# The portions in which feed-forward steps are given out, from unit 8 on, computed from a group's columns

## The chip, the core and the metric

The kernel runs on one core of a Trainium2 chip. It has five engines with a queue each: TensorE (PE in the profile; its weight loads are PEld), VectorE (DVE), ScalarE (ACT), GpSimd (POOL), and SyncE (SP), which here only issues DMAs. The metric is the device time of one execution in microseconds, as the median of several runs.

## What is computed

Attention first: 4 batches, 8 heads, 768 tokens, 48 features. Each head keeps a 48 x 48 state that is decayed by a gate for every feature and gains an outer product for every token:

```python
f = 1.0 / (1.0 + np.exp(-f_logit))
for t in range(S):
    state = f[:, :, t, :, None] * state + np.einsum('bhd,bhe->bhde', k[:, :, t], v[:, :, t])
    y[:, :, t] = np.einsum('bhd,bhde->bhe', q[:, :, t], state)
```

The result is read as x with 3072 tokens of 384 features and goes through a feed-forward network (FFN) with three first matrices of 384 x 768 and one output matrix of 768 x 384:

```python
h = np.maximum(np.maximum(x @ w1, x @ w2), x @ w3)
return h @ w_out
```

All of it is in float32.

## The kernel before

**Units and groups.** The attention works on units of 64 tokens of two batches, 24 in all (NU). Four units (GRP) make a group of 512 tokens (TOK), and the FFN works on one group at a time; its six groups are numbered 0 to 5. The FFN of a group can begin when the attention of its four units is done, so the FFN of group g runs beside the attention of group g + 1, and that of the last group runs alone at the end.

**A unit of attention.** `sigmoids(u)` (L308, ACT) gives the gates, `scan(u)` (L326, VectorE) their running products, `after(u)` and `before(u)` scale k and q by them to kh and qh (L337 and L348; from unit 8 on, POOL). `keys(u)` does nothing from unit 8 on; `keys_by_blocks(u, n)` (L379, VectorE) transposes kh in four parts, n = 0 to 3. `pairs(u)` multiplies kh and qh (L389, PE), and VectorE masks the product to `at` (L392). `values(u)` multiplies `at` with v (L408, PE) and calls `sums(u)` (L433, PE), which forms the new part of the state from the transposed keys and v; VectorE adds it (L441). `carry(n)` decays the state for the next unit (L354, POOL). `finish(u)` adds what the state gives (L503, PE) and copies the sum into the group's xT (L509, ACT). `pack` moves a part of xT to the place where the FFN reads it, with two DMAs (L522). The last two units (22 and 23) need no transposed keys and no L433.

**The FFN of a group.** `ffn(g)` is a generator. Its first part has twelve products of 512 columns, three matmuls each (L551); for each j there are two products, the first followed by a Relu on ACT (L749), the second by a maximum on VectorE into hm (L751). For the last three j, POOL forms sums of hm (L608, four operations for each j). The second part, `outputs_by_pairs`, has eleven steps, in each of which `into` runs twice with three matmuls of 192 columns (L623, 66 matmuls in all). Behind some of the steps ACT or VectorE copies or adds the result out of its bank (L634, L637, L639, L643, L646, L651, L659); the bank is used again by a later step. The stores of a group's outputs are issued by `store_late`, in the next group.

**What sets the order.** The program is written under a manual schedule: each engine runs its instructions in the order in which the Python code emits them. The loop over the units calls the parts of the attention and, between them, `fill(PART)` five times for each unit. `fill(ns)` adds ns to a budget and takes steps of the pending generators as long as the budget is over zero; each step yields its cost, which is columns times COLUMN = 4/2.4 ns. A step that overshoots leaves a negative budget for the next call, and what is left over when nothing is pending stays in the budget. At the start of a group, behind the first `fill` of unit 8, 12, 16 or 20, `finish` of the last unit of the group before is called, then `pack`, and then `ffn` of that group is appended to the pending generators; at the end the same is done for unit 23, and `fill(20000)`, `fill(9000)` and `fill(10 ** 6)` give out the rest. What is still pending from the group before comes first. The FFN of group 0 (`ffn_first`) is given out beside units 3 to 8.

From unit 11 on there are also checks of the weights' range on ACT (L276, L277, L279), two for each unit.

Of the kernel before, what the change touches and what calls it, by code (L numbers as in the profile page):

```python
# [55 lines left out]
def kernel(  # L56
# [18 lines left out]
    NK = DM // 128  # L75
    DFF = moe_w1.shape[1]
    NJ = DFF // 128
    GRP = 4
    TOK = GRP * UT
# [10 lines left out]
    def fast():  # L90
        ctx = ExitStack()
        with ctx:
# [95 lines left out]
            def load_v(u, queues=one):  # L188
                load_tokens(v_tiles[u % NLD], v, u, queues)
# [19 lines left out]
            def load_weights(count, done=0, queue=nc.sync):  # L209

                for n in range(len(raw_next), min(len(raw_next) + count, done + RAW, len(pieces))):
                    raw_next.append(n)
                    dst, src = pieces[n]
                    a = dst.shape[1]
                    if src.dtype != FP32:
                        raw[n] = new_raw(n)
                        dst, src = raw[n].rearrange("p (a c) -> p a c", a=a), src.bitcast(U32)
                    queue.dma_start(out=dst, in_=src.rearrange("(a p) c -> p a c", a=a))
# [308 lines left out]
            COLUMN = 4 / 2.4  # L527
# [59 lines left out]
            HJ, HD = NJ // 2, DM // 2  # L587
# [177 lines left out]
            def fill(ns):  # L765
                budget[0] += ns
                while budget[0] > 0 and pending:
                    try:
                        budget[0] -= next(pending[0])
                    except StopIteration:  # L770
                        pending.pop(0)
# [8 lines left out]
            def new_xT():  # L780
                return work.tile([128, HP, TOK], FP32, name="xT")

            CHECKS = 2 * GRP + 3
            STEP = NK * HALF * COLUMN
            PART = 2740

# [1 line left out]
            with tc.manual_schedule():  # L790
                load(0, both)
                load(1, (nc.scalar, nc.sync))
                load_v(0)
                load(2, one, "f")
                load_v(1)
                load(2, one, "kq")
                load(3)
                load_weights(3)
                load_v(2)
                load_v(3)  # L800
                load_weights(6)
                xT = new_xT()
                sigmoids(0)
                scan(0)
                after(0)
                before(0)
                sigmoids(1)
                keys(0)
                scan(1)
                after(1)  # L810
                pairs(0)
                before(1)
                sigmoids(2)
                busy(1)
                values(0)
                y_by_tokens(0)
                keys(1)
                sums(0)
                load(GRP)
                load_v(GRP)  # L820
                scan(2)
                after(2)
                pairs(1)
                x_of_tokens(0, xT)
                carry(2)
                before(2)
                sigmoids(3)
                busy(1)
                values(1)
                y_by_tokens(1)  # L830
                keys(2)
                sums(1)
                round_begin(0)
                round_end(0)
                x_of_tokens(1, xT)
                scan(3)
                pairs(2)
                round_begin(1)
                round_end(1)
                after(3)  # L840
                carry(3)
                round_begin(2)
                pending.append(ffn_first(xT))
                fill(STEP)
                before(3)
                values(2)
                fill(STEP)
                keys(3)
                sums(2)
                y_by_tokens(2)  # L850
                pairs(3)
                fill(STEP)
                x_of_tokens(2, xT)
                fill(STEP)
                values(3)
                fill(STEP)
                sums(3)
                fill(STEP)
                y_by_tokens(3)
                load(GRP + 1)  # L860
                load_v(GRP + 1)
                x_of_tokens(3, xT)
                sigmoids(GRP)
                scan(GRP)
                after(GRP)
                fill(2 * STEP)
                before(GRP)
                carry(GRP)
                fill(2 * STEP)
                for u in range(GRP, NU):  # L870
                    n = u + 1
                    fill(PART)
                    keys(u)
                    keys_by_blocks(u, 2)
                    if u > GRP:
                        finish(u - 1, xT)
                        if u % GRP == 3:
                            pack(0, 2, xT)
                        elif u % GRP == 0:
                            pack(3, 3, xT)  # L880
                    if u % GRP == 0:
                        if u > GRP:
                            pending.append(ffn(u // GRP - 1, xT))
                        xT = new_xT()
                    pairs(u)

                    if u + 2 < BY_ROWS:
                        load(u + 2)
                    if BY_ROWS <= u + 3 < NU and u % 2:
                        load(u + 3, one, "fkq" if u % GRP == 1 else "f")  # L890
                    if u + 2 < NU:
                        load_v(u + 2)
                    if n < NU:
                        sigmoids(n)
                        scan(n)
                    if CHECKS <= u < CHECKS + len(pieces) // 2:
                        check_range(2 * (u - CHECKS))
                    fill(PART)
                    keys_by_blocks(u, 3)
                    if n < NU:  # L900
                        after(n)
                        before(n)
                    fill(PART)
                    if BY_ROWS <= u + 2 < NU and u % GRP == 0:
                        load(u + 2, one, "k")
                    values(u)
                    if n < NU:
                        carry(n)
                    if CHECKS <= u < CHECKS + len(pieces) // 2:
                        check_range(2 * (u - CHECKS) + 1)  # L910
                    fill(PART)
                    if CHECKS <= u + 2 < CHECKS + len(pieces) // 2:
                        check_load(2 * (u + 2 - CHECKS))
                        check_load(2 * (u + 2 - CHECKS) + 1)
                    if BY_ROWS <= u + 2 < NU and u % GRP == 0:
                        load(u + 2, one, "q")
                    keys_by_blocks(n, 0)
                    fill(PART - 1000 if u < 2 * GRP else PART)
                    keys_by_blocks(n, 1)
                fill(PART)  # L920
                finish(NU - 1, xT)
                pack(3, 3, xT, both)
                pending.append(ffn(NU // GRP - 1, xT))
                fill(20000)

                least = work.tile([128, 1], FP32, name="least")
                nc.vector.tensor_reduce(out=least, in_=ends.rearrange("p u a -> p (u a)"), op=ALU.min, axis=AX.X)
                nc.vector.tensor_scalar(least, least, P_MIN, None, op0=ALU.is_lt)
                most = work.tile([128, 1], FP32, name="most")
                nc.vector.tensor_reduce(out=most, in_=outside, op=ALU.max, axis=AX.X)  # L930
                nc.vector.tensor_scalar(most, most, 0.0, None, op0=ALU.is_gt)
                fill(9000)
                n_low = ps_tr.tile([1, 1], FP32, name="tr")
                nc.tensor.matmul(n_low, lhsT=least, rhs=is_feature, start=True, stop=False)
                nc.tensor.matmul(n_low, lhsT=most, rhs=causal[:, 127:128], start=False, stop=True)
                nc.vector.tensor_copy(low, n_low)
                engines = (nc.sync, nc.scalar, nc.gpsimd, nc.vector, nc.tensor)
                tc.mark_branch_hint_location("rare", "LikelyTaken", [e.engine for e in engines])
                fill(10 ** 6)

    def general():
# [5 lines left out]
        with ctx:  # L947
# [194 lines left out]
            for u in range(NU):  # L1142
# [5 lines left out]
                if u % GRP == GRP - 1:  # L1148
                    ffn(u // GRP, xT)

    fast()
    n_low = nc.values_load(low[0:1, 0:1], min_val=0, max_val=256)

# [32 lines left out]
```

## Time and profile before

| | |
|---|---|
| median of 3 runs | 450.65 us (450.5 to 452.4) |
| profiled execution, own time | 452.01 us |
| its span, first to last instruction | 450.3 us |
| mean granted clock of TensorE | 0.987 |
| PE, DVE, ACT, POOL busy, 130 to 193 us | 63.00, 47.60, 18.77, 25.53 us |
| the same, 193 to 255 us | 62.00, 44.33, 22.81, 25.49 us |
| the same, 255 to 320 us | 64.57, 46.43, 25.47, 25.77 us |
| the same, 320 to 385 us | 62.66, 28.83, 22.60, 21.61 us |
| the same, 385 to 450.3 us | 56.01, 6.14, 6.87, 9.43 us |

The stretches are about those of the groups: the FFN of group 1 begins at 135 us, that of group 2 at 197, of group 3 at 258, of group 4 at 323 and of group 5 at 388. Busy time is that of an engine's instructions, its waits left out. A matmul in float32 appears as two records, so that twelve records of 192 columns are six matmuls. A wait is put down to the engine that the profile shows to have come last; where a wait is for several, it may have been another.

### The profile page before, as it was taken

The numbers are of one execution on the slowest core, as the hardware profiler recorded it, in microseconds if no ns is written. First come the engines' busy times: TensorE is split into PE (matmuls) and PEld (weight loads), VectorE is DVE, ScalarE is ACT, GpSimd is POOL, SyncE is SP. The second block draws the span as 40 slices with busy tenths as digits, with TensorE's granted clock in tenths as the row PEclk, the third lists the DMA queues.
The fourth block names the chain that finished last, engine by engine and source line by source line (L and its number), as shares of the span: only waits on it lengthen the run. The fifth ranks groups of instructions, "written<-read, shape, count | busy, mean of one in ns | idle before, by whom it ended". The sixth has DMA issues, their size and how long they took to land.

```text
span 450.3 us, 10831 instructions
## 1 busy us (share of the span) xinstructions
PE 426.1 (95%) x4362; PEld 286.1 (64%) x4362; DVE 264.1 (59%) x526; ACT 152.6 (34%) x361; POOL 152.5 (34%) x190
## 2 busy tenths in 40 slices
PE   4989999998999999999999999999899999699994
PEld 3777755555664448965469954489645599344694
DVE  6975677873585898478688468768467320011100
ACT  2433747504312214325425415424325321111010
POOL 2153643610330376232374133464033550002400
PEclk9999999999999999999999999999999999699999
DMA  8999987107766643376754276745273000300002
GB/s 168 221 272 325 259 169 90 30 21 161 120 101 86 110 128 52 92 141 116 98 158 75 84 141 110 91 158 108 65 160 59 1 1 15 76 0 0 1 1 74
DMA packets 174070, 46.56 MB, mean 103 GB/s; under 512 B 153856, under 2 KB 171712, under 8 KB 174016
## 3 DMA queue, kind: packets, MB, share of 16 engines
q1 hardware_dynamic: 170672, 45.02, 48.3%
q10 hardware_dynamic: 3344, 0.81, 0.8%
q8 instruction: 35, 0.57, 0.5%
q14 instruction: 19, 0.16, 0.1%
HBM read 37.75 MB, written 4.72 MB: 94 GB/s over the span
## 4 chain that ended last, share of the span: by engine, by line
PE 84%; DVE 5%; ACT 3%; DMA 3%; issue 2%; SPq 2%; POOL 0%; DVEq 0%; ACTq 0%
PE p L551 25%; PE tr L551 18%; PE tr L623 13%; PE p L623 11%; PE p L695 3%; PE y L408 3%; PE y L503 2%; PE a L389 2%; DMA f_ld<-in_f_logit_dram 2%; PE p L574 2%; PE y L433 2%; SPq L464 1%; DVE w_in L678 1%; PE y L404 1%; DVE r L326 1%
## 5 line engine op out<-in xcount | busy, mean ns | idle before, releaser
L551 PE MATMUL tr<-xT,placed 128*128 128x512 f32 x180 | 86.0, 612 | 3.4 <-DMA xT<-xT 3.4
L551 PE MATMUL p<-xT,placed 128*128 128x512 f32 x180 | 84.7, 600 | 2.1 <-ACT rest_bits L279 2.1
L379 DVE STREAM_TRANSPOSE ks<-kh 32x128 f32<-32x128 f32 x224 | 67.6, 302 | 3.5
L551 PEld LDWEIGHTS tr<-xT,placed 128*128 128x128 f32 x180 | 34.4, 194 | 44.0 <-issue 43.4
L551 PEld LDWEIGHTS p<-xT,placed 128*128 128x128 f32 x180 | 33.5, 191 | 40.4 <-issue 37.4
L551 PE MATMUL p<-xT,w_in 128*128 128x256 f32 (+1 forms) x144 | 51.7, 504 | 1.7 <-DVE hm L715 1.4
L336 POOL COPY ends<-r 128x8 f32<-128x8 f32 x24 | 6.7, 278 | 121.6 <-DVE r L326 121.6
L392 DVE TENSOR_TENSOR at<-a,mask 128x512 f32<-128x512 f32 x24 | 16.6, 690 | 48.8 <-PE a L389 48.8
L337 POOL TENSOR_TENSOR kh<-kt,r 128x512 f32<-128x512 f32 x16 | 30.4, 1898 | 30.0 <-DVE kt L293 30.0
L551 PEld LDWEIGHTS p<-xT,w_in 128*128 128x128 f32 x144 | 26.8, 197 | 17.6 <-issue 13.5
L509 ACT COPY xT<-y 64x256 f32<-64x256 f32 (+1 forms) x60 | 22.1, 368 | 40.4 <-PE y L503 39.8
L751 DVE TENSOR_TENSOR hm<-p,top 128x512 f32<-128x512 f32 x18 | 12.2, 680 | 39.6 <-PE p L551 39.6
L749 ACT ACTIVATE top<-tr 128x512 f32<-128x512 f32 x18 | 10.7, 596 | 69.8 <-PE tr L551 69.8
L326 DVE TENSOR_TENSOR_SCAN r<-gate,from_one 128x520 f32<-128x520 f32 x24 | 30.1, 1255 | 5.8 <-ACT gate L305 2.8
L608 POOL TENSOR_TENSOR w_in<-hm 128x256 f32<-128x256 f32 x15 | 10.8, 722 | 66.2 <-DVE hm L751 63.9
L344 DVE TENSOR_TENSOR_SCAN prod<-gate,from_inv 128x520 f32<-128x520 f32 x24 | 30.6, 1275 | 0.0
L256 POOL TENSOR_TENSOR w_in<-top_bits,rest_bits 128x384 uint32<-128x384 uint32 x18 | 20.7, 1161 | 28.3 <-DVE top_bits L250 13.8
L623 PE MATMUL tr<-w_in,xT 128*128 128x192 f32 x132 | 23.4, 328 | 0.0
L623 PEld LDWEIGHTS tr<-w_in,xT 128*128 128x128 f32 x132 | 21.6, 190 | 0.2
L348 POOL TENSOR_TENSOR qh<-qt,prod 128x512 f32<-128x512 f32 x16 | 19.3, 1207 | 0.0
L623 PE MATMUL p<-w_in,xT 128*128 128x192 f32 x108 | 19.1, 328 | 0.0
L354 POOL TENSOR_TENSOR state<-st,ends 128x384 f32<-128x384 f32 x22 | 18.8, 857 | 0.2
(153 smaller groups left out, 671.4 us busy)
## 6 DMA issues: line engine op xcount, KB each, us to landing
raw<-in_moe_w_dram SPq DMA_DIRECT2D x30, 384.0 KB, 5.3
v_ld<-in_v_dram SPq DMA_DIRECT2D x48, 96.0 KB, 3.3
out_dram<-o SPq DMA_DIRECT2D x46, 96.0 KB, 2.4
placed<-in_moe_w_dram SPq DMA_DIRECT2D x6, 384.0 KB, 6.2
placed<-in_moe_w_out_dram SPq DMA_DIRECT2D x6, 384.0 KB, 4.5
raw<-in_moe_w_out_dram SPq DMA_DIRECT2D x6, 384.0 KB, 4.4
f_ld<-in_f_logit_dram SPq DMA_DIRECT2D x32, 64.0 KB, 2.7
k_ld<-in_k_dram SPq DMA_DIRECT2D x32, 64.0 KB, 2.7
```

The source lines that it names most:

```text
L256: nc.gpsimd.tensor_tensor(dst, by(top), by(rest), op=ALU.add)
L326: nc.vector.tensor_tensor_scan(r[:, 0:LEN][:, ::-1], flat(gate)[:, ::-1], flat(from_one)[:, ::-1], 1.0, op0=ALU.mult, op1=ALU.max)
L337: (nc.vector if u < BY_ROWS else nc.gpsimd).tensor_tensor(kh.rearrange("p h a t -> p a h t"), kt, by_batch(r[:, 1:LEN + 1].rearrange("p (x ...
L344: nc.vector.tensor_tensor_scan(flat(prod), flat(gate_tiles[u % 2]), flat(from_inv[u % 2]), 1.0, op0=ALU.mult, op1=ALU.max)
L348: (nc.vector if u < BY_ROWS else nc.gpsimd).tensor_tensor(qh, qt, by_batch(prod[:, :, 1:]), op=ALU.mult)
L354: nc.gpsimd.tensor_tensor(t, states[u % 2], ends[:, u, :].unsqueeze(2).to_broadcast([128, 2 * HP, D]), op=ALU.mult)
L379: nc.vector.transpose(ks[n * 32:(n + 1) * 32, :, par, e0:e0 + 32], kh[p0:p0 + 32, :, a, t0:t0 + 32])
L392: nc.vector.tensor_tensor(at, p[:, :, 0:HP * C].rearrange("s par (h t) -> s par h t", h=HP), mask.unsqueeze(1).unsqueeze(1).to_broadcast([ ...
L408: nc.tensor.matmul(y[o:o + DP, a, hp * C:(hp + 1) * C], lhsT=v_ld[s, 2 * hp + par, :], rhs=d["at"][s, par, hp, :], start=(hp == 0), stop=F ...
L509: nc.scalar.copy(xT[o, :, t0 + a * C:t0 + (a + 1) * C], y[i, a, 0:HP * C].rearrange("p (h t) -> p h t", h=HP))
L551: nc.tensor.matmul(p if g or w < TOK else p.rearrange("p (two t) -> p two t", two=2), lhsT=weight(g, i)[:, kt, j * 128:(j + 1) * 128], rhs ...
L623: nc.tensor.matmul(bank[:, p * HD:(p + 1) * HD], lhsT=lhs(p)[:, k], rhs=rhs[:, k], start=id(bank) not in begun, stop=(k == HJ - 1), skip_g ...
```

## The change

The portion is no longer the constant 2740 from unit 8 on, but a twentieth (5 calls for each of 4 units) of the cost of a group's FFN steps: twelve products of 3 matmuls with 512 columns, and 22 calls of `into` with 3 matmuls of 192 columns. That comes to 2592. The units 4 to 7 keep 2740. The single `fill(PART)` behind the loop takes the new value too.

```diff
-            PART = 2740
+            EARLY = 2740
+            PART = (NJ * 2 * NK * TOK + 22 * HJ * HD) * COLUMN / (5 * GRP)
...
                 for u in range(GRP, NU):
                     n = u + 1
-                    fill(PART)
+                    part = EARLY if u < 2 * GRP else PART
+                    fill(part)
...
-                    fill(PART)
+                    fill(part)
                     keys_by_blocks(u, 3)
...
-                    fill(PART)
+                    fill(part)
...
                     values(u)
...
-                    fill(PART)
+                    fill(part)
...
                     keys_by_blocks(n, 0)
-                    fill(PART - 1000 if u < 2 * GRP else PART)
+                    fill(part - 1000 if u < 2 * GRP else part)
                     keys_by_blocks(n, 1)
                 fill(PART)
                 finish(NU - 1, xT)
```

## The prediction

> **What bounds the kernel now.** I read the page first (busy rows and slices), then TensorE's waits from 130 us on, where the change acts, then the chain of waits, then the timelines around each wait.
>
> ```profile
> PE 426.1 (95%) x4362; PEld 286.1 (64%) x4362; DVE 264.1 (59%) x526; ACT 152.6 (34%) x361; POOL 152.5 (34%) x190
> ...
> PE   4989999998999999999999999999899999699994
> ...
> PEclk9999999999999999999999999999999999699999
> ```
>
> TensorE (PE) is the bound: full in nearly every slice, VectorE next at 59%. Slice 34 (382.8 to 394.0 us) stands out, in work and in clock. So the change can gain only what TensorE stands idle or runs slow, and lose only where it makes TensorE wait. The waits of PE from 130 us to the end:
>
> ```profile
> PE tr L551 <- DMA xT<-xT: 3.4, 1, 3.4
> PE p L551 <- ACT rest_bits L279: 2.1, 1, 2.1
> PE tr L623 <- DVE o L659: 0.5, 1, 0.5
> PE tr L623 <- ACT w_in L639: 0.4, 1, 0.4
> ```
>
> Four waits, 6.4 us together (total, times, longest). The first is in the chain of waits at the end of the attention part (start, us, what):
>
> ```profile
> 384.13 0.64 PE y L503 x32
> ...
> 385.96 2.06 DMA xT<-xT
> 388.03 0.14 issue
> 388.16 5.46 PE tr L551 x6
> 393.62 2.71 PE p L551 x6
> 396.34 2.58 PE tr L551 x6
> ```
>
> finish(23) ends at 384.77; ACT copies its result (L509), a DMA packs it (L522), and only then can the last group's first product start. Its six records (three matmuls) take 5.46 us where the same six take 2.58 later: the clock had been halved by the wait.
>
> The second wait, 321.51 to 323.57, is the same thing one group earlier, at finish(19): the pack's issues run from 320.72 to 322.03 and a pack takes 1.9/2.3/2.7 us to land, so the 323.54 at which PE was released is the DMA; the ACT line named just ended then. The fourth, at 307.01, is the ACT copy L639, queued behind finish(18)'s copies, the next unit's sigmoid and a range check (ACT is busy without a break from 303.06 to 306.96). The third belongs to the final output steps.
>
> **What the Trainium skill says.** "TensorE: Matmul & The Clock Gate", Part 1: after an idle window of about 3.4 us the clock falls to half until a busy window has passed. The trace agrees: 3.44 us idle, then 5.46 for 2.58; the 2.06 us wait cost no clock (next six records 2.81). Same page, "Architectural detail": ScalarE and VectorE queues are strictly first in, first out; the copy L639 waiting behind the checks agrees. "DMA: Bandwidth & Descriptors", "Anatomy of one DMA — SWDGE (gpsimd) path": about 2.0 us fixed per transfer. These packs go by another path, and the trace has 2.3 for them, which I use.
>
> **The change, part by part.** The new portion is (6·2·3·512 + 22·3·192)·(4/2.4)/20 = 31104·1.667/20 = 51840/20 = 2592 ns. One group of four units calls fill 20 times, so a group's allowance is now exactly its products; before it was 20·2740 = 54800, 2960 ns too much. That surplus eats what is still pending when the next group is appended. The order of PE's instructions in the changed program shows it. Matmuls of 0.325 us (L623) left over behind finish(11), (15), (19), (23): before 21, 12, 3, 0, that is 6.8, 3.9, 1.0 and 0 us of cover for the pack; after 33 each time, 33·0.325 = 10.7 us. No instruction is added or removed; only places in the queues change, and only from unit 8.
>
> *Removed.* The pack needs about 3.4 us from the end of finish, against 10.7 us of cover. So go: the wait at 384.8 (3.44), the slow clock behind it (5.46 − 2.58 = 2.88), and the wait at 321.5 (2.06). The wait for L639 (0.43) goes too: between step s2·w_mix1 and the step that rewrites its bank no unit boundary falls now. Sum 8.81 us. The 0.5 in the final outputs stays.
>
> *What falls on the boundary instead.* Since a group's allowance is exact, all groups are now cut alike. In units 12, 16, 20 finish comes inside the sixth step (hm·w_mix2), and ACT copy L646 is queued behind finish's copies, sigmoid and check, free 4.1 us after the first L503 (302.39 to 306.50). Its product is ready at 1.06+0.19+0.98+1.95 = 4.2; copy 0.48, done by about 4.8; PE comes back to that bank after one more step (1.95), at 6.1. Slack 1.3 us: cost 0.
>
> *Added.* L433 needs all four transposes of keys_by_blocks(u, 3) on VectorE. These come after at (L392), gate, scan, reciprocal, and sometimes an hm maximum (L751). Before's unit 9 has just that order (VectorE):
>
> ```profile
> 140.05 0.69 DVE L392 TENSOR_TENSOR at<-a,mask 128x512 f32<-128x512 f32 x1 [4.32 <-PE a L389]
> 141.39 0.71 DVE L293 STREAM_TRANSPOSE gate<-sig 128x512 f32<-128x512 f32 x1 [0.65 <-ACT sig L308]
> 142.14 1.24 DVE L326 TENSOR_TENSOR_SCAN r<-gate,from_one 128x520 f32<-128x520 f32 x1
> 143.41 0.21 DVE L329 RECIPROCAL from_inv<-r 128x8 f32<-128x8 f32 x1
> 143.53 0.64 DVE L751 TENSOR_TENSOR hm<-p,top 128x512 f32<-128x512 f32 x1
> 144.21 1.28 DVE L379 STREAM_TRANSPOSE ks<-kh 32x128 f32<-32x128 f32 x4
> ```
>
> and TensorE beside it:
>
> ```profile
> 138.85 0.67 PE L503 MATMUL y<-qh,state 48*48 48x64 f32 x32
> ...
> 145.26 0.69 PE L408 MATMUL y<-at,v_ld 64*64 64x64 f32 x32
> 145.77 0.63 PE L433 MATMUL y<-v_ld,ks 64*64 64x48 f32 x32
> ```
>
> The keys end at 145.49, 6.64 us after the first L503, L433 came at 6.92: no wait. In the new order, units 11, 15 and 19 have between L389 and L408 one matmul of 512 columns and nine of 192, and VectorE again has L751 ahead of the keys. PE: L503 and L389 1.06, one matmul with the switch 1.05, nine at 0.325 = 2.93, L408 0.62: L433 is reached at 5.66. The keys end at 6.64. PE waits 1.0 us, three times: 3.0 us (unit 23 needs no keys). Bounds for one: 0, if the chain on VectorE runs 1 us ahead of unit 9's, and 1.7, if ACT's part of the chain runs 0.7 later. I take 1.0. Behind the waiting L433 stand the products; VectorE's state update (L441) waits too, but is not needed before the next finish.
>
> The other units: 9, 13, 17, 21 have six matmuls of 512 columns there, L433 at 1.06+0.19+5.15+0.62 = 7.0 against keys at 6.64 plus some 0.1 for a Relu (L749) ahead of finish's copies: 0. Units 10, 14, 18 have eight: 8.7 against about 7: 0. kh and qh on POOL: in before's unit 19 qh is done 10.0 us after the first L503; the shortest new unit (11, 15, 19) is 14.1 without its wait, and the four-operation sums ahead (2.9) still leave 1 to 2 us: 0. Moved on SP: the eight output stores come behind the next loads of f, k and q, which are issued two units before use; 0. The last group has the same steps as before.
>
> *Sum.* 452.01 (profiled execution; span 450.3 and 1.71 around it) − 8.81 + 3.0 = 446.2 us. The median of the runs is 450.65, the profiled execution at the upper end of 450.5 to 452.4. The half-clock stretch may differ from run to run; it disappears in either, so I keep the 446.2 as the absolute time and do not scale it.
>
> **The rivals.**
> A. *L433 never waits* (the keys come in time, the wait is worth 0): 452.01 − 8.81 = 443.2. For it: the slack is within 1 us. Against: VectorE's order and unit 9's times.
> B. *The gain is eaten* by the same wait, larger: each chain 0.7 us later gives 1.7·3 in units 11, 15, 19 and 0.5·4 in units 9, 13, 17, 21 = 7.1, so 450.3. For: in units 9, 13, 17 and 21 a Relu (L749, 0.60) stands ahead of finish's copies on ACT, which start the chain. Against: it can start as its product ends, with L503, and holds the copies up by 0.1 only; in units 11, 15 and 19 there is none.
> C. *Slower*: POOL becomes the bound in units 11, 15, 19. There the sums of hm for two columns (8 operations of 0.72 = 5.8 us), then ends 0.19, kh 1.96 and qh 1.17 stand in one row before the next L389. If the second sum starts as late as 8.7 (behind the transpose of q instead of before the keys) qh is done at 14.9 where L389 wants it at 14.7: from there on every us costs three. Above 452.9 (6.7 over the forecast) takes 2.3 us more in each. Against: VectorE's order has L751 ahead of the keys, so the sum can start at 5.3, and POOL is busy 25.5 of 62 us around there.
> D. *It doesn't do what it says*: excluded by the order, 33 left-over matmuls at each of the four boundaries.
>
> **How the numbers follow.** A difference under 0.5% (448.4 to 452.9) can't be told from no change here. Chances: forecast 0.57 (444.5 to 447.5), A 0.18, B 0.16 (two parts in a hundred of it still under 448.4), C 0.09. Range: from A's 443.2, with 0.4 for other small waits that may go, to 449.2, half of B: 442.8 to 449.2. Faster 0.57 + 0.18 + 0.02 = 0.77, same 0.14, slower 0.09.
>
> **What would show it.** In the changed trace: no PE wait at L551 for the pack, and no slice of PEclk under 9 behind finish(23); 33 L623 matmuls between finish and the first L551 of each group; PE waits at L433 for VectorE's L379 (3 times, about 1.0 us; none for A, seven for B); no wait at L623 for L646; none at L389 for POOL (C). The prediction is wrong if the end of the last L503 is followed by idle time, or if PE from 130 us on idles over 6 us.

## The result and the profile after

The changed kernel takes 445.53 us (median, 444.46 to 446.84), before 450.64: ratio 0.9879, 95% interval 0.9837 to 0.9921. It is faster by 1.2%. Its profiled execution took 444.46 us with a span of 442.6.

The page of the changed kernel, the same rows as shown of before:

```profile
PE 423.5 (96%) x4362; PEld 285.2 (64%) x4362; DVE 264.9 (60%) x526; ACT 153.0 (35%) x361; POOL 152.4 (34%) x190
...
PE   4989999998999999999999999999999999999994
...
PEclk9999999999999999999999999999999999999998
```

Slice 34 no longer stands out: TensorE is full up to the last slice, and its clock with it. The numbers of instructions are the same as before. TensorE's waits from 130 us on (engine, line and what it waited for; total us, times, longest):

```profile
PE y L433 <- DVE ks L379: 1.7, 6, 0.3
PE tr L623 <- DVE o L659: 0.5, 1, 0.5
```

Both pack waits at L551 and the one for L639 are gone; a new one at L433 has come. The chain of waits around finish(23) (start, us, what):

```profile
372.23 0.59 PE y L503 x32
372.82 10.92 PE p L623 x66
383.74 2.57 PE tr L551 x6
386.32 2.58 PE p L551 x6
```

Behind finish's L503 stand 66 records, 33 matmuls, of group 4. They last 10.92 us. The pack lands under them (its two DMAs are issued at 373.67 and 374.06 and take 1.9 and 2.0 us to land), and the last group's first product runs at once and at full clock (2.57).

**The two profiled executions don't start level.** Up to the first L503 of finish(7) TensorE's instructions are the same in both kernels, but before reaches it at 121.70 us and the changed one at 119.97. This 1.73 us is no part of the change (the section on the experiments finds its cause). So what the change did is read from that L503 to the end of the span: before 450.3 − 121.70 = 328.60, after 442.6 − 119.97 = 322.63, a gain of 5.97 us. All experiments are measured by this stretch too; "stretch" below means it.

### The profile page after: what moved, and what is told of

It is laid out like the page before. It is cut to its first block, busy times and chain, and to the rows that moved or that the text cites. A ratio compares the mean times of both kernels' runs of the same rounds, so it can differ in the third digit from the quotient of the medians.

```text
span 442.6 us, 10849 instructions
## 1 busy us (share of the span) xinstructions
PE 423.5 (96%) x4362; PEld 285.2 (64%) x4362; DVE 264.9 (60%) x526; ACT 153.0 (35%) x361; POOL 152.4 (34%) x190
## 4 chain that ended last, share of the span: by engine, by line
PE 84%; DVE 6%; ACT 3%; DMA 2%; issue 2%; SPq 2%; POOL 0%; ACTq 0%; DVEq 0%
PE p L551 26%; PE tr L551 18%; PE tr L623 13%; PE p L623 10%; PE p L695 3%; PE y L503 2%; PE y L408 2%; DMA f_ld<-in_f_logit_dram 2%; PE y L433 2%; PE a L389 2%; PE p L574 2%; SPq L464 1%; DVE w_in L678 1%; PE y L404 1%; PE tr L288 1%
## 5 line engine op out<-in xcount | busy, mean ns | idle before, releaser
L551 PE MATMUL p<-xT,placed 128*128 128x512 f32 x180 | 84.1, 599 | 0.0
L551 PE MATMUL tr<-xT,placed 128*128 128x512 f32 x180 | 83.8, 598 | 0.0
L551 PEld LDWEIGHTS tr<-xT,placed 128*128 128x128 f32 x180 | 33.3, 190 | 37.7 <-issue 36.4
L551 PEld LDWEIGHTS p<-xT,placed 128*128 128x128 f32 x180 | 33.2, 190 | 37.5 <-issue 36.6
L551 PE MATMUL p<-xT,w_in 128*128 128x256 f32 (+1 forms) x144 | 50.3, 492 | 1.7 <-DVE hm L715 1.4
L337 POOL TENSOR_TENSOR kh<-kt,r 128x512 f32<-128x512 f32 x16 | 29.1, 1816 | 28.6 <-DVE kt L293 28.6
L551 PEld LDWEIGHTS p<-xT,w_in 128*128 128x128 f32 x144 | 25.9, 190 | 17.4 <-issue 13.3
L751 DVE TENSOR_TENSOR hm<-p,top 128x512 f32<-128x512 f32 x18 | 12.2, 676 | 29.0 <-PE p L551 29.0
```

The source lines that it names most:

```text
L337: (nc.vector if u < BY_ROWS else nc.gpsimd).tensor_tensor(kh.rearrange("p h a t -> p a h t"), kt, by_batch(r[:, 1:LEN + 1].rearrange("p (x ...
L551: nc.tensor.matmul(p if g or w < TOK else p.rearrange("p (two t) -> p two t", two=2), lhsT=weight(g, i)[:, kt, j * 128:(j + 1) * 128], rhs ...
```

## The experiments

The theory is that of the prediction: the gain is work left over behind finish, which covers the pack ("cover"), and the price is the wait at L433. The rival: it is the evenness of the portions that gains.

**Cover without even portions.** The constant 2740 stays; the surplus is taken off once per group, behind `values`:

```diff
                         check_range(2 * (u - CHECKS) + 1)
+                    if u % GRP == 0 and u > 2 * GRP:
+                        budget[0] -= 2960
                     fill(PART)
```

> The constant 2740 of before, but the surplus of a group (2960 ns) is taken off the budget once in each of the units 12, 16 and 20, behind values. So 21 matmuls of 192 columns (6.8 us) stay behind finish(11), (15), (19) and (23), and L433 is nowhere reached before its keys (6.75 to 7.9 us after the first L503, keys at 6.0 to 6.6). Measured from the first L503 of finish(7), which comes before anything changes (before 328.5, changed kernel 322.6 us to the end). Theory 'cover' (the gain is work left over behind finish, the price is the wait at L433): all pack waits go, no L433 wait, 319.1 us, about 442 in all. Rival 'even portions' (the gain comes from portions that fill the group evenly): the portions are as uneven as before, so 327 to 328.5, about 450.

Measured: 441.81 us, ratio 0.9787 (0.9753 to 0.982) to before; stretch 439.1 − 120.03 = 319.07. From 130 us on TensorE has one wait left, the 0.5 in the last outputs. The chain around finish(23) in this version:

```profile
372.63 0.59 PE y L503 x32
373.23 7.02 PE p L623 x42
380.25 2.58 PE tr L551 x6
```

21 matmuls are cover enough. Uneven portions bring more than even ones, so the rival falls. By the theory, the 3.5 us by which this version beats the change are the price of where the even portions put L433; the next experiment tests that.

**That price by itself.** The changed kernel with the four transposes emitted earlier:

```diff
                     pairs(u)
+                    keys_by_blocks(u, 3)
...
                     fill(part)
-                    keys_by_blocks(u, 3)
```

> The changed kernel with keys_by_blocks(u, 3) emitted right behind pairs(u), so that VectorE does the four transposes behind the mask (L392) and before the gate, scan and hm maximum. Theory 'cover and L433': the keys end about 3.1 us after the first L503, the waits at L433 in units 11, 15 and 19 (1.2 us of lost TensorE time each) go, 319.1 us from the first L503 of finish(7), 3.5 us faster than the changed kernel. Rival: the transposes hold up gate and scan by 0.65 us in every unit and that comes back as a wait at L389 or at L503: no gain, 322.6 or more.

Measured: 442.07 us, ratio 0.9786 (0.9751 to 0.9822); stretch 440.7 − 121.61 = 319.09. No wait at L433 is left, and no other took its place. So the L433 waits cost 322.63 − 319.09 = 3.54 us, 1.18 in each of the three units.

The profile counts only 1.7 us of idle time for them. Why the price is double shows in TensorE's timeline of the changed kernel in unit 11:

```profile
172.98 0.69 PE L408 MATMUL y<-at,v_ld 64*64 64x64 f32 x32
173.50 0.27 PE L433 MATMUL y<-v_ld,ks 64*64 64x48 f32 x4
173.99 0.31 PE L433 MATMUL y<-v_ld,ks 64*64 64x48 f32 x2 [0.23 <-DVE ks L379]
174.65 0.66 PE L433 MATMUL y<-v_ld,ks 64*64 64x48 f32 x26 [0.34 <-DVE ks L379]
175.24 1.24 PE L623 MATMUL p<-w_in,xT 128*128 128x192 f32 x6
```

For comparison, the same place in before's unit 9, where nothing waited:

```profile
145.26 0.69 PE L408 MATMUL y<-at,v_ld 64*64 64x64 f32 x32
145.77 0.63 PE L433 MATMUL y<-v_ld,ks 64*64 64x48 f32 x32
146.34 1.12 PE L551 MATMUL p<-xT,placed 128*128 128x512 f32 x2
```

And VectorE in unit 11 of the changed kernel:

```profile
172.64 0.65 DVE L751 TENSOR_TENSOR hm<-p,top 128x512 f32<-128x512 f32 x1
173.31 1.28 DVE L379 STREAM_TRANSPOSE ks<-kh 32x128 f32<-32x128 f32 x4
174.62 0.71 DVE L293 STREAM_TRANSPOSE kt<-k_ld 128x512 f32<-128x512 f32 x1
```

L433 isn't held back as a whole. Its first four records need no key that is late; the next two wait 0.23, the rest 0.34, each for its own transpose. From the first record (173.50) to the 26 that come last (174.65) 1.15 us pass. Only 0.57 of them stand as idle time, since the six records between the waits count 0.58 as busy. But these six save nothing: from 174.65 to the next product it is 0.59 us, in unit 9 the whole row of 32 took 146.34 − 145.77 = 0.57. From L408's start to the next product it is 175.24 − 172.98 = 2.26 us; in unit 9 it was 146.34 − 145.26 = 1.08, and the same 1.08 in unit 11 with the transposes emitted earlier. The difference, 1.18, is the true loss, and the same as the experiment's. Start to start tells more here than the idle time.

**The last border alone.** 2740 up to unit 19, 2400 from unit 20 on (the edit is that of the change with `PART = 2400` and `u < NU - GRP` in place of `u < 2 * GRP`).

> The constant 2740 up to unit 19 and 2400 from unit 20 on: only the last border gets cover (18 matmuls of 192 columns, 5.9 us, behind finish(23); 6 instead of 3 behind finish(19)). Theory 'cover': the last pack wait (3.44) and the half clock behind it (2.88) go, and 1.0 of the wait behind finish(19): 328.5 - 7.3 = 321.2 us from the first L503 of finish(7), so more than the whole net gain of the change from its last four units. Rival 'even portions': at most a fifth of the gain, 327 or more.

Measured: 443.91 us, ratio 0.9834 (0.98 to 0.9867); stretch 441.5 − 120.08 = 321.42. Of the waits from 130 us on, 1.1 us of the pack wait behind finish(19) and the 0.4 for L639 are still there, as expected. So 328.60 − 321.42 = 7.2 us come from the last four units alone, of the 9.5 that the version with the surplus taken off gains. Touching only these beats the whole change, since this version has no wait at L433. The rival, 327 or more, falls here too.

**The cover used up again.** In the changed kernel, the single fill behind the loop is made larger:

```diff
-                fill(PART)
+                fill(PART + 10900)
                 finish(NU - 1, xT)
```

> The changed kernel, but the single fill behind the loop gives out 10900 ns more, so that nothing is left behind finish(23); all else is as in the changed kernel. Theory 'cover': the pack wait (3.4) and the half clock (2.9) are back: 322.6 + 6.3 = 328.9 us from the first L503 of finish(7), as slow as before. If the half clock depends on where the wait falls[...], 326 to 328.9. Rival 'even portions': 322.6.

Measured: 450.39 us, ratio 0.9971 (0.9957 to 0.9986); stretch 447.9 − 120.05 = 327.85. One fill call takes 5.2 of the 5.97 us back, and the rival's 322.6 falls. The chain of waits:

```profile
383.05 0.64 PE y L503 x32
...
384.88 2.01 DMA xT<-xT
386.89 0.14 issue
387.03 4.10 PE tr L551 x6
391.12 2.99 PE p L551 x6
394.11 2.58 PE tr L551 x6
```

The wait (3.4) is back as it was in before; the half clock costs 4.10 + 2.99 − 2·2.58 = 1.93 us, in before 5.46 + 2.71 − 5.16 = 3.01. So in these two traces the wait costs the same and the clock does not, which is why 327.85 was reached instead of the 328.9 of a full price. The granted clock shows why: behind finish(23) it is 0.50 in before from about 386.95 to 393.78 us, here only from about 388.40 to 391.83. The 22 runs of this kernel spread from 447.94 to 452.33; a part of that is the early 1.7 us treated below. The fastest, with a mean clock of 0.997, is about what the wait alone would give (an estimate: the changed kernel's fastest run, 444.46, and the wait of 3.4 make 447.9), so in that run the clock was perhaps not halved at all.

**A shorter wait.** The same edit with 8300, which leaves 6 of the 33 matmuls.

> The changed kernel, but the single fill behind the loop gives out 8300 ns more, so that 6 of the 33 matmuls (1.95 us) stay behind finish(23). Theory 'wait and clock are two prices': TensorE waits 3.4 - 1.95 = 1.45 us for the pack, too short to halve the clock: 322.6 + 1.45 = 324.1 us from the first L503 of finish(7), and the first six records of L551 take about 2.8. Rival 'any wait there halves the clock': 326 or more, with first records above 4 us.

Measured: 446.01 us, ratio 0.9879 (0.9851 to 0.9907); stretch 445.8 − 121.65 = 324.15.

```profile
384.53 1.99 DMA xT<-xT
386.52 0.14 issue
386.66 2.81 PE tr L551 x6
389.47 2.58 PE p L551 x6
```

The profile counts 1.2 us of idle time; the stretch is 1.52 longer than the changed kernel's. The first six records take 2.81, and the granted clock is 1.00 from 385 to 400 us, so the clock was not halved behind this wait. The rival, 326 or more, falls. Wait and clock are two prices.

**The early 1.73 us.** The runs of most versions fall on two levels: the changed kernel has 444.46 and 444.58 with a mean clock of 0.997 and 0.996, but 446.84 and 446.48 with 0.992. The version with the surplus taken off has 440.9 to 441.05 and 442.57 to 443.39. TensorE's timeline of before around 30 us:

```profile
28.32 0.68 PE L433 MATMUL a<-v_ld,ks 64*64 64x48 f32 x32
30.47 0.19 PE L476 MATMUL p<-st 128*1 128x1 f32 x2 [1.47 <-DVE st L441]
30.59 0.68 PE L481 MATMUL y<-state,qh 48*64 48x48 f32 x32
31.09 0.66 PE L389 MATMUL a<-qh,kh 48*64 48x64 f32 x32
31.68 2.68 PE L551 MATMUL p<-xT,w_in 128*128 128x256 f32 x6
```

and that of the changed kernel's last line there:

```profile
31.64 1.56 PE L551 MATMUL p<-xT,w_in 128*128 128x256 f32 x6
```

Same wait, same instructions, but in one execution the clock is halved behind it (from 32 to 40 us the granted clock is 0.79 in before and 1.00 in the changed kernel). Seven of the kept traces have this wait: three (before, the earlier keys, the shorter wait) show the half clock, the other four don't. The profiled execution of the shorter wait, 447.51 us, is also one of the two slower runs of its kernel (447.51 and 447.66, the others 445.9 to 446.07). Two edits to the version with the surplus taken off go at this place: four matmuls without use ahead of `y_by_tokens(2)`, or a real FFN step there:

```diff
                 sums(2)
+                busy(4)
                 y_by_tokens(2)
```

> The version with the surplus taken off, and four matmuls of 256 columns without use ahead of y_by_tokens(2), where TensorE idles 1.47 us at about 29 us (for the state, L441), long before the change acts. Theory: the two levels of the runs (mean clock 0.997 and 0.992, some 1.8 us apart) come from the clock being halved behind this idle time in some executions. Then all runs have 0.997 and lie within 0.6 us, near 441.2 (440.9 to 441.05 of the fast level, plus 0.3 for the matmuls that overshoot). Rival: the level is set elsewhere; runs still lie 1.8 us apart.

```diff
                 sums(2)
+                fill(STEP)
                 y_by_tokens(2)
                 pairs(3)
-                fill(STEP)
```

> The version with the surplus taken off, and the fill(STEP) that stands behind pairs(3) put ahead of y_by_tokens(2), so that a real FFN step covers the 1.47 us for which TensorE waits for the state. If that wait is on the path: 1.0 to 1.5 us faster than the version with the surplus taken off, 439.5 to 440 us, and, by the theory of the halved clock, all runs on one level at 0.997 or above. Rival: pairs(3) and the chain behind it come later by as much, so the time is that of the version with the surplus taken off.

Measured: 441.67 us for the first (441.28 to 442.2, where the version without it had 440.9 to 443.39) and 439.78 for the second (439.63 to 440.25). The two levels are gone in both, six runs each, with mean clocks of 0.994 to 0.999. The first keeps 0.9 us of spread, more than the 0.6 expected, and its median is 0.5 above the 441.2 expected; why, these runs don't tell. The second also takes the wait itself off the path; its first L503 of finish(7) comes at 118.78, and its stretch is 437.9 − 118.78 = 319.1, that of the version it builds on. At a ratio of 0.9738 (0.9712 to 0.9763) to before it is the fastest version tried, 5.75 us under the changed kernel's median and 4.7 under its fastest run (444.46); what it gains over the version it builds on lies before finish(7).

## Why the prediction was right

Forecast 446.2 us, measured 445.53. That these two numbers lie so close is in part luck. The forecast was made against the profiled execution of before, which had the early half clock; the changed kernel's runs on that level are 446.48 and 446.84, and the median falls between the two levels because two of four runs are on each. For the stretch, where the level drops out, −8.81 + 3.0 = −5.81 was predicted, and −5.97 measured. Here the mechanism is right, but two errors of size offset each other, as shown below.

*The bound and where the gain lies.* Right. TensorE is the bound; the four units before the end hold most of it, as the edit of the last border alone shows.

*Removed.* Each of the four terms went: pack wait 3.44, half clock 2.88, pack wait behind finish(19) 2.06, L639 0.43. Filling the last border again brought wait and clock back, and part of the cover brought the wait alone. The 2.88 for the half clock is what it cost in the one execution that was profiled; with the cover used up the same wait cost 1.93 in clock, so a forecast made from an execution like that one would have put the gain about 1 us lower (an estimate from these two numbers).

*Costed at nothing.* L646 in units 12, 16 and 20, the chain to kh and qh on POOL, the L433 of all other units and the moved stores: none of them shows as a wait of TensorE in the changed trace.

*Added.* The place was right (units 11, 15 and 19, VectorE's L751 ahead of the keys; L433's last records began at 174.65, 6.71 us after the L503 at 167.94, where 6.64 was estimated for the keys). The size was 1.0 and is 1.18, 3.54 instead of 3.0 in all. The loss is the time by which the row is late, as was assumed; that time was put at 6.64 − 5.66 = 0.98. L433 was reached 5.56 us after the L503, 0.1 earlier than reckoned, and the last records began 0.07 later than the keys' end that was estimated, which makes 1.15.

*What makes up the sum.* −8.81 + 3.54 = −5.27, and −5.97 was measured. The 0.7 us come mostly from pricing before's waits by their idle time. Start to start in TensorE's timelines they cost more:

| | put at | in before | the same work without the wait | cost |
|---|---|---|---|---|
| wait behind finish(19) | 2.06 | 320.27 to 326.22, 5.95 | surplus taken off, 3.65 | 2.30 |
| wait for L639 | 0.43 | 304.46 to 309.16, 4.70 | surplus taken off, 4.00 | 0.70 |
| last border, wait and half clock | 6.32 | 384.06 to 398.75, 14.69 | changed kernel, 8.32 | 6.37 |

That is 9.37 where 8.81 was put. The end adds 0.26: from the last VectorE addition to the end of the span it takes 450.3 − 444.73 = 5.57 us before and 442.6 − 437.29 = 5.31 after. −9.37 + 3.54 − 0.26 = −6.09, which is 0.12 from the measured −5.97. So the waits that went were worth 0.56 more than the prediction said, and the new one cost 0.54 more. That these two errors offset each other is luck.

*The rivals.* A (no wait at L433, 443.2) falls: the wait is in the trace and costs 3.54 us. B would have it in seven units; there are three. C would show as a wait at L389 for POOL; there is none from 130 us on. D falls by the 33 matmuls.

## What to carry to other kernels

Where background work is handed out in portions beside a chain, the portions need not be even; there must be enough left at the points where the bounding engine would otherwise wait for a copy and a transfer. Count what is left at each such point in the order of instructions, and count also what the new cut puts ahead of the next instruction with a deadline: a second cut (the surplus taken off in one place) had cover enough without the new wait and gained 3.5 us more. Price a wait by start to start against an undisturbed unit, not by the idle time shown.

## What the runs showed of the hardware

The prediction reads the 3.44 us of idle time in before as agreeing with a rule that the clock falls behind an idle window of about that length. The traces are less simple.

*When it falls.* Behind finish(23) of before, TensorE is idle from 384.72, and the granted clock is halved from about 386.95 on, after 2.2 us. With the cover used up, TensorE works again from 387.03, and the half clock begins at about 388.40, 1.4 us later. At 29 us, 1.47 us of idle time between rows of small matmuls (48 to 64 rows and columns) was followed by the half clock in three traces and not in four, though the instructions up to there are the same; filling that idle time removed it. A wait of 2.06 us between denser matmuls (before, at 321.5) and one of 1.22 (the shorter wait) had none in the one trace of each. So the idle time alone doesn't say whether the clock falls; what else decides, these runs don't show.

*What it costs.* The half clock lasted about 3.4 us at the early place in before (31.98 to 35.38) and with the cover used up (388.40 to 391.83), and about 6.8 us, twice as long, at the last border of before (386.95 to 393.78). Only work under it is slowed: half of the time in which TensorE worked at half clock is 1.7, 1.7 and (393.78 − 388.16) / 2 = 2.8 us, against prices of 1.73, 1.93 and 3.01 read from the stretches and records.
